# Turning 320 of 480 channels of the inverse spectrum by DMA through DRAM, in a replanned order, in a gated long-convolution and gMLP kernel

## The chip, the cores and the metric

The kernel runs on one core of a Trainium2 chip. A core has the engines PE (TensorE, matmul), DVE (VectorE), ACT (ScalarE), POOL (GpSimd) and SP (SyncE), which issue their instructions in order, each from its own queue, and share 16 DMA engines. The metric is the device time of one execution in microseconds (us); lower is better. Times are compared as medians of several executions.

## The reference

For x of 2048 positions and 640 channels the output is a mix of two branches, `g * a + (1 - g) * b`, with the gate `g = sigmoid(sum(x * gate_w))` per position.

Branch a is a long convolution of every channel with its own kernel of 2048 taps, which is itself computed from 128 complex modes per channel:

```python
P = jnp.exp(logdA[:, :, None] * l[None, None, :])
K = jnp.einsum('dn,dnl,dn->dl', Cc, P, dB).real
Kf = rfft of K padded to 4096;  Uf = rfft of u padded to 4096
y  = irfft(Uf * Kf)[first 2048] + u * Dskip
```

Branch b is a gMLP block: `z = gelu(x @ w_in)`, cut into halves of 864; the second half goes through a layernorm over channels, is mixed over positions by the 2048 x 2048 matrix `w_sp` plus `b_sp`, multiplied by the first half, and goes through `w_out`.

## The kernel before, in words

**Branch b** is `z2_tile` and `z1_tile` (projection and gelu; z1 goes to DRAM) and `sp_block`, eight blocks of 256 positions each: the mixing matmuls ps_g (L810), the gating on DVE (vT, L814 and L816), and the output projection ps_o (L830), rescaled into `acc` or `ob` (L834).

**Branch a** is a Fourier transform in two stages, done as matmuls with tables. The 640 channels are handled as two groups, `h=0` with 480 channels and `h=1` with 160. Exponentials and tables (`k_exps`, `k_tables`: ACT and DVE) feed `k_sub` (ps_k, L1043 and L1044), which gives factors of the kernel K. They go to DRAM (`KA_d`, `KB_d`), and `k_expand` loads them back in repeated form, 27 transfers for each group, into `xk`. `conv_s1` is stage 1 of K: matmuls ps_s1k (L1132), evacuated to bf16 by ACT or DVE (L420), stored to `FK_d`. `s1_u` does the same for the input (`FU_d`). The turn of axes between the stages is the trip through DRAM: `conv_s2` loads `fu` and `fk` back with other axes in the partitions.

`conv_s2` runs over 32 blocks of frequencies: one at a time for 480 channels (32 products in all), two at a time for 160 (16 products). For each step PE makes ps_u (L1179) and ps_s2k (L1186), ACT copies ps_u to `us` (L420), DVE multiplies ps_s2k by `us` (the product p, L1188), PE turns the product back by the first inverse stage (ps_v, L1194), and ACT copies ps_v into `vs[h]` (L1196), a bf16 tile of 128 partitions x 32 blocks x 480 or 160 channels.

`conv_vt` then turns `vs` in place. Within every group of 32 partitions the partition index and the block index change places. This is done by DVE with STREAM_TRANSPOSE (L1202) on 40 channels at a time, taken as 20 float32 pairs: 12 such operations for 480 channels and 4 for 160. Each needs all blocks of its group. `conv_i2` is the last inverse stage: matmuls with the table HT over the turned `vs` (L1278 for 480, L1276 for 160), half of them added to the output by DVE (L1210), half scaled by ACT (tm, L1227) and added by DVE or POOL (L1229); then the output goes out from SP. A block of `conv_i2` needs all turns of its group.

**What sets the order.** Nothing is ordered at run time. The class `Plan` collects all operations as tasks, with an assumed cost, the buffers that they read and write, and a priority: the longest remaining path, plus a bias, plus an entry of the table `TUNE`, keyed by function and line offset. `Plan.run` then simulates the engines, with one serial DMA channel and a fixed landing time for each transfer, and writes down a static sequence for each engine. A task whose engine is given as several (evacuations: ACT or DVE; transfers: `QQ`, SP or POOL) is given to one of them by this simulation. A change of `TUNE` or of an assumed cost therefore changes the order on all engines, and where such tasks run, and nothing of what is computed. The semaphore waits follow from the tiles that an instruction reads and writes in the emitted order; two accesses to one tile are ordered when their address ranges overlap.

Around the change: the `fu` and `fk` loads stand on SP only and have three buffers each; the transfers of `k_expand` and the stores to `FK_d` are on SP or POOL. The regions of memory for the second group (`cv1`) are opened once the first group's stage 1 is done.

Of the kernel before, what the change touches and what calls it, by code (L numbers as in the profile page):

```python
# [13 lines left out]
BF = mybir.dt.bfloat16  # L14
# [11 lines left out]
class Handle:  # L26
# [9 lines left out]


TUNE = {
    ('conv_s1', 15, ('g', 1)): 3463,
    ('conv_s2', 43, ('h', 0)): 2566,  # L40
    ('conv_s2', 34, None): 6794,
    ('conv_s2', 27, ('h', 1)): 252,
    ('conv_s2', 10, None): 10339,
    ('conv_s2', 14, ('h', 0)): 1700,
    ('conv_s2', 42, None): 26749,
    ('eights', 6, None): 35100,
    ('eights', 13, None): 2232,
    ('i2_out', 7, None): -1101,
    ('k_exps', 10, None): -17175,
    ('k_store', 13, None): -4187,  # L50
    ('k_store', 14, None): -20275,
    ('k_sub', 13, None): -11680,
    ('k_tables', 31, None): 12165,
    ('k_tables', 32, ('c', 2)): -15072,
    ('k_tables', 32, ('c', 6)): -5826,
    ('k_tables', 32, None): -8380,
    ('k_tables', 30, None): -26683,
    ('k_tables', 29, ('c', 7)): -19807,
    ('k_tables', 29, None): -21734,
    ('k_tables', 18, ('c', 7)): 1753,  # L60
    ('k_tables', 18, None): -14417,
    ('k_tables', 17, ('c', 3)): 17782,
    ('k_tables', 36, ('c', 6)): -8483,
    ('k_tables', 36, ('c', 7)): -31949,
    ('k_tables', 20, ('c', 1)): -27268,
    ('k_tables', 20, ('c', 4)): -2369,
    ('k_tables', 20, None): 1822,
    ('k_tables', 21, ('c', 4)): -3380,
    ('k_tables', 38, ('c', 2)): 2234,
    ('k_tables', 38, ('c', 6)): 23056,  # L70
    ('k_tables', 38, None): 275,
    ('k_tables', 23, None): 2152,
    ('main', 160, None): 9405,
    ('main', 350, None): -821,
    ('main', 151, ('g', 0)): 23897,
    ('main', 151, None): 1843,
    ('main', 149, None): 6466,
    ('main', 370, None): -29957,
    ('main', 365, None): -6662,
    ('main', 435, None): -1293,  # L80
    ('main', 415, None): -9571,
    ('main', 412, None): 12264,
    ('main', 443, None): -165,
    ('main', 411, None): -19156,
    ('main', 419, None): -2698,
    ('ob_load', 7, None): -17373,
    ('quads', 6, None): -20516,
    ('s1_u', 13, ('h', 1)): 20716,
    ('s1_u', 13, ('n0', 10)): -22604,
    ('s1_u', 16, None): -19744,  # L90
    ('s1_u', 3, ('n0', 0)): -12146,
    ('s1_u', 3, None): -2641,
    ('s1_u', 18, ('h', 1)): -36848,
    ('s1_u', 14, ('n0', 2)): 280,
    ('s1_u', 14, None): -34357,
    ('sp_block', 20, ('tb', 0)): 14608,
    ('sp_block', 20, ('tb', 1)): 2295,
    ('sp_block', 20, ('tb', 2)): 1783,
    ('sp_block', 20, ('tb', 7)): -4631,
    ('sp_block', 20, None): -28643,  # L100
    ('sp_block', 42, ('tb', 4)): -2761,
    ('sp_block', 42, None): -1053,
    ('sp_block', 47, None): -23570,
    ('sp_block', 3, ('tb', 0)): 4184,
    ('sp_block', 3, ('tb', 7)): -12304,
    ('sp_block', 3, None): -2466,
    ('sp_block', 8, None): -13804,
    ('sp_block', 6, ('tb', 2)): -1163,
    ('sp_block', 6, ('tb', 4)): -19214,
    ('sp_block', 6, None): -2088,  # L110
    ('sp_block', 5, ('tb', 2)): -12744,
    ('sp_block', 5, ('tb', 7)): -13832,
    ('z1_tile', 10, ('g', 1)): -8523,
    ('z1_tile', 10, None): 3231,
    ('z1_tile', 15, ('g', 0)): 2499,
    ('z1_tile', 15, None): -2684,
    ('z2_tile', 18, ('h', 1)): -15976,
    ('z2_tile', 18, None): 9745,
}
HELPERS = ("dma", "actf", "evac", "<lambda>", "ptt", "pts", "ftt", "fts", "pstt", "S_", "E", "K_", "M_")  # L120

# [1 line left out]
class Plan:  # L123
# [51 lines left out]
    def run(self):  # L175
# [26 lines left out]
        dma = 0.0  # L202
# [9 lines left out]
        while len(order) < N:  # L212
# [10 lines left out]
            while again:  # L223
                again = False
                for e in self.ENG:
# [3 lines left out]
                    for i in ready[e]:  # L229
                        if done[i] or rdy[i] > now + 1e-9:  # L230
                            continue
                        t = T[i]
                        ok = True
                        for h in t["hs"]:
# [3 lines left out]
                            n = self.rings[h.ring]  # L238
# [16 lines left out]
                    t = T[best]  # L255
                    i = best
# [3 lines left out]
                    c = t["costs"][t["engs"].index(e)]  # L260
# [15 lines left out]
                    if t["nb"]:  # L276
                        s = max(end + (0.0 if t["hold"] else 1.0), dma)
                        dma = s + t["nb"] / 1e6
                        fin = dma + (2.2 if t["hold"] else 0.9) + (0.9 if e == "POOL" else 0.0)
                        if t["hold"]:  # L280
                            end = dma
                    else:
                        fin = now + c + self.LAT.get(e, 0.0)
# [35 lines left out]
def kernel(  # L319
# [20 lines left out]
    P = 128  # L340
# [35 lines left out]
    dram = ctx.enter_context(tc.tile_pool(name="dram", bufs=1, space=DRAM))  # L376
    GW, GO = (480, 160), (0, 480)
    FU_d = [dram.tile([16, 4, 2, 32, w], BF, name=f"FU_d{w}") for w in GW]
    FK_d = [dram.tile([16, 4, 2, 32, w], BF, name=f"FK_d{w}") for w in GW]
    KA_d = [dram.tile([16, NB, w], BF, name=f"KA_d{w}") for w in GW]  # L380
    KB_d = [dram.tile([129, w], BF, name=f"KB_d{w}") for w in GW]
    z1_d = dram.tile([8, P, NFT, 256], BF, name="z1_d")
# [17 lines left out]
    def dma(q, out_, in_, nb, r=(), w=(), tr=False, bias=0.0, deps=(), run=640):  # L400

        qs = (q,) if isinstance(q, str) else q

        def fn(e):
            if tr:
                E_[e].dma_start(out=out_(), in_=in_(), transpose=True)  # L406
            else:
                E_[e].dma_start(out=out_(), in_=in_())
        return add(qs, [0.67 if tr else QC[x] + (0.3 if run < 250 and x == "SP" else 0.0) for x in qs], fn, r=r, w=w, nbytes=max(nb * 3.64e-6 if tr else nb / run * (20 + run / 27.2) / 16000, 0.001) * 1e6, hold=tr, bias=bias, deps=deps)
# [159 lines left out]
    X = {}  # L569
# [515 lines left out]
    def k_expand(h):  # L1085
        W = GW[h]
        xk = sbt((CVA, CV1)[h], f"xk{h}", "xk", [P, NS, W])
        rx = [("cva", "cv1")[h]]
        KA, KB = KA_d[h], KB_d[h]
        rd = KAB[h]  # L1090
        pieces = []

        def mk(src, dims):
            return bass.AP(src.tensor, src.offset, dims + [list(src.ap[-1])])
        x3 = lambda: xk()[:].rearrange("p (e r) d -> p e r d", e=2)

# [12 lines left out]
        wk = [[] for _ in range(NS)]  # L1109
        for i, (n0, rep, rows_, dst, src) in enumerate(sorted(pieces, key=lambda t: t[0])):  # L1110
            for n in range(n0, n0 + rep):
                wk[n].append((xk, i))
            dma(QQ, dst, src, rows_ * 2 * W, r=rd + rx, w=[(xk, i)], bias=8000 - 5 * i, run=2 * W)
        return xk, wk

    cva_ids = []
# [36 lines left out]
    def conv_s2(h):  # L1153
        W = GW[h]
# [5 lines left out]
        for k in range(0, 32, NK):  # L1160
# [33 lines left out]
                        pe.matmul(pv()[:, W * n:W * n + W], lhsT=GV(k + n, i), rhs=p12()[:, i, W * n:W * n + W], start=(i == 0), stop=(i == 1))  # L1194
            mv_id[h] = add("PE", 2 * NK * mm(W), mv_, r=[p12, gk], w=[pv], bias=S2B + 200)
            add("ACT", 0.15 + NW / 1170, lambda e, k=k, pv=pv: act.copy(out=X["vs"][h][:, k:k + NK, :], in_=pv()[:, 0:NW].rearrange("p (k d) -> p k d", k=NK)), r=[pv, "cvb"], w=[("vs", h, k)], bias=S2E)  # L1196

    def conv_vt(g):
        h = g // 3
# [47 lines left out]
    def conv_i2(h, oo):  # L1247
        W, dsl = GW[h], slice(GO[h], GO[h] + GW[h])
        nn = (1, 2)[h]
        for u, n in enumerate(range(0, NS, 2 * nn)):  # L1250
# [28 lines left out]
            if u == 0:  # L1279
# [95 lines left out]
```

## Time and profile before

| | |
|---|---|
| median of 8 runs | 357.6 us |
| runs, lowest to highest | 353.97 to 359.53 us |
| the profiled execution | 358.57 us, its span 356.8 us |
| mean TensorE clock granted | 0.964 |
| PE, DVE, ACT, POOL busy | 312.8, 282.5, 248.7, 85.8 us |
| moved by DMA | 59.89 MB, 168 GB/s |
| hardware queue, software queue | 62.7% and 6.5% of the 16 engines' span |
| first and last product of 480 channels (L1188) | starts at 266.7, ends at 305.9 us |
| turns on DVE (L1202) | 16, 18.7 us |

The profile is of one execution; all positions below are microseconds from the start of its span. "Busy" does not count the issue of DMAs, waits or branches. In the chain a line gives the start, the length and the work or the wait; in a group of instructions the columns after the bar are the busy time, the mean length of one in ns, and the idle time before them. "issue" is time in which an engine waited for nothing that the profile shows. A DMA time "to landing" runs from the issue to the completion.

### The profile page before, as it was taken

Reading aid. Unit: us, or ns where it says so; the run is one execution under the profiler, and the core shown is the slowest. Engines: PE = TensorE matmul, PEld = TensorE weight load, DVE = VectorE, ACT = ScalarE, POOL = GpSimd, SP = SyncE. Lnnn points to the kernel's source line nnn. Section 1 sums busy time; section 2 is a strip of 40 time slices with the busy share of each in tenths; the row PEclk is TensorE's granted clock in tenths of the full one; section 3 lists DMA queues with packets and bytes.
Section 4 is the critical chain, followed back from the end, with each engine's and each line's share of the span. In section 5 each row is a group of like instructions: output and inputs, shape, how many; then the busy total and the mean of one; then the engine's idle time right before and its main releaser. Section 6 shows DMA issues by size and latency. Waiting matters only on the chain.

```text
span 356.8 us, 8362 instructions
## 1 busy us (share of the span) xinstructions
PE 312.8 (88%) x3237; PEld 217.0 (61%) x3237; DVE 282.5 (79%) x554; ACT 248.7 (70%) x445; POOL 85.8 (24%) x108
## 2 busy tenths in 40 slices
PE   3899797988999999999999999499999999809982
PEld 3454353676775787878966988277775333406751
DVE  4049896597899789996699699237678999996985
ACT  1877666799999678889967574136648888804842
POOL 3002766000000000000270064436478000203220
PEclk9999999899999999999999999689999999976998
DMA  7989886757686669689088337977969786273404
GB/s 206 203 137 216 154 223 146 205 144 162 175 227 164 172 123 242 153 212 203 27 115 156 93 78 138 171 189 219 274 183 276 197 253 175 63 209 135 140 28 129
DMA packets 108848, 59.89 MB, mean 168 GB/s; under 512 B 76730, under 2 KB 105194, under 8 KB 108810
## 3 DMA queue, kind: packets, MB, share of 16 engines
q1 hardware_dynamic: 106218, 54.46, 62.7%
q0 software_dynamic: 2592, 4.91, 6.5%
q8 instruction: 25, 0.41, 0.5%
q14 instruction: 13, 0.11, 0.1%
HBM read 25.25 MB, written 19.47 MB: 125 GB/s over the span
## 4 chain that ended last, share of the span: by engine, by line
PE 28%; DVE 27%; ACT 18%; SPq 10%; DMA 7%; POOL 5%; issue 5%; ACTq 0%; DVEq 0%
PE ps_g L810 10%; ACT mr L413 9%; SPq L406 8%; DVE p L1188 6%; DVE vs L1202 5%; PE ps_z L622 4%; PE ps_o L830 4%; ACT L413 2%; PE ps_s2k L1186 2%; ACT ET L413 2%; DMA xk<-KA_d 2%; PE ps_v L1194 2%; DMA FK_d<-s1k 2%; POOL phi L359 2%; PE ps_s1k L1132 2%
## 5 line engine op out<-in xcount | busy, mean ns | idle before, releaser
L810 PE MATMUL ps_g<-wT,z2n 128*128 128x256 bf16 (+1 forms) x896 | 107.7, 275 | 4.0 <-DVE vT L814 2.1
L810 PEld LDWEIGHTS <-z2n 128*128 128x128 bf16 (+1 forms) x896 | 89.5, 102 | 20.9 <-issue 5.4
L1188 DVE TENSOR_TENSOR p<-ps_s2k,us 128x960 bf16<-128x960 f32 (+1 forms) x48 | 48.7, 1043 | 4.1 <-ACT us L420 1.5
L991 POOL COPY ET<-mr 128x80 bf16<-128x80 bf16 x7 | 6.0, 853 | 135.9 <-PE ps_k L1044 129.2
L830 PE MATMUL ps_o<-Wout,vT 128*128 128x320 bf16 (+1 forms) x224 | 34.0, 299 | 2.2 <-ACT s1u L420 1.8
L622 PE MATMUL ps_z<-xg,Win 128*128 128x512 bf16 (+1 forms) x140 | 33.3, 393 | 2.7 <-ACT zt L413 2.7
L590 PE MATMUL ps_z<-Win,xT 128*128 128x432 bf16 (+1 forms) x160 | 30.5, 347 | 2.0 <-ACT gl L596 2.0
L413 ACT ACTIVATE ET<-ci 128x640 bf16<-128x640 int16 (+1 forms) x40 | 25.7, 681 | 7.0 <-DVE ci L359 7.0
L1044 PE MATMUL ps_k<-ET 128*32 128x33 bf16 x640 | 28.0, 258 | 2.7 <-issue 2.7
L1043 PEld LDWEIGHTS <-ET 128*32 128x32 bf16 x640 | 27.0, 192 | 4.7 <-issue 4.4
L830 PEld LDWEIGHTS <-vT 128*128 128x128 bf16 (+1 forms) x224 | 21.8, 97 | 12.3 <-issue 3.2
L1196 ACT CAST vs<-ps_v 128x480 bf16<-128x480 f32 (+1 forms) x48 | 24.8, 520 | 5.0 <-PE ps_v L1194 4.7
L1043 PE MATMUL ps_k<-ET 128*32 128x33 bf16 x640 | 28.2, 259 | 0.0
L1044 PEld LDWEIGHTS <-ET 128*32 128x32 bf16 x640 | 27.4, 195 | 0.0
L1194 PE MATMUL ps_v<-p,G 128*128 128x480 bf16 (+1 forms) x128 | 25.6, 304 | 1.6 <-DVE p L1188 0.8
L814 DVE TENSOR_TENSOR vT<-ps_g,br 128x512 bf16<-128x512 f32 (+1 forms) x32 | 18.8, 617 | 10.1 <-PE ps_g L810 10.1
L622 PEld LDWEIGHTS <-Win 128*128 128x128 bf16 (+1 forms) x140 | 14.6, 104 | 19.4 <-issue 5.7
L420 ACT CAST us<-ps_u 128x480 bf16<-128x480 f32 (+1 forms) x48 | 24.5, 520 | 2.1 <-ACT vs L1196 0.9
L1186 PE MATMUL ps_s2k<-fk,T 128*128 128x480 bf16 (+1 forms) x128 | 25.4, 309 | 0.4 <-DMA fk<-FK_d 0.3
L590 PEld LDWEIGHTS <-xT 128*128 128x128 bf16 x160 | 15.5, 98 | 15.9 <-issue 2.5
L413 ACT ACTIVATE mr<-lre 128x320 bf16<-128x320 f32 x66 | 24.8, 456 | 0.0
L420 ACT CAST s1k<-ps_s1k 128x960 bf16<-128x960 f32 (+1 forms) x16 | 13.4, 860 | 13.0 <-PE ps_s1k L1132 10.1
(193 smaller groups left out, 588.6 us busy)
## 6 DMA issues: line engine op xcount, KB each, us to landing
FU_d<-s1u SPq DMA_DIRECT2D x16, 240.0 KB, 2.8
fu<-FU_d SPq DMA_DIRECT2D x16, 240.0 KB, 3.7
fk<-FK_d SPq DMA_DIRECT2D x16, 240.0 KB, 4.1
z_d<-zt SPq DMA_DIRECT2D x24, 128.0 KB, 1.9
z1t<-z_d SPq DMA_DIRECT2D x8, 384.0 KB, 4.4
xf<-in_A_u_dram SPq DMA_DIRECT2D x8, 320.0 KB, 3.3
Win<-in_B_w_in_dram SPq DMA_DIRECT2D x2, 1080.0 KB, 5.7
ob_d<-ob SPq DMA_DIRECT2D x12, 160.0 KB, 4.2
```

What stands on the lines that cost most here:

```text
L406: E_[e].dma_start(out=out_(), in_=in_(), transpose=True)
L413: return add("ACT", cost, lambda e: act.activation(out=out_(), in_=in_(), func=func, scale=scale), r=r, w=w, fset=fs, bias=bias, deps=deps ...
L420: (vec.tensor_copy if e == "DVE" else act.copy)(out=out_(), in_=in_())
L590: pe.matmul(ps()[:, h, 0:432 + h], lhsT=xT[:, i, 128 * st:128 * st + 128], rhs=Win2[:, i, 432 * h:432 * h + 432 + h], start=(i == 0), stop ...
L622: pe.matmul(ps()[0:fs, ft - f0, :], lhsT=Win1[:, i, 128 * ft:128 * ft + fs], rhs=xg()[:, i, :], start=(i == 0), stop=(i == ND - 1))
L810: pe.matmul(ps()[0:fs, ft - f0, :], lhsT=z2n[:, st, 128 * ft:128 * ft + fs], rhs=wT()[:, st, :], start=(st == 0), stop=(st == NS - 1))
L830: pe.matmul(ps()[:], lhsT=vT[ft // 2]()[0:fs, ft % 2, 128 * r:128 * r + 128], rhs=Wout[0:fs, ft, HD * h:HD * h + HD], start=(ft == 0), sto ...
L1043: pe.matmul(o_, lhsT=ET[:, 0:32, d], rhs=M2[:, :, d], start=True, stop=False, tile_position=(0, 32 * q))
L1044: pe.matmul(o_, lhsT=ET[:, NA:NA + 32, d], rhs=E2[:, :, d], start=False, stop=True, tile_position=(0, 32 * q))
L1186: pe.matmul(ps()[:, i, W * n:W * n + W], lhsT=TK(k + n, i), rhs=fk()[:, j + n, :], start=True, stop=True)
L1188: add("DVE", dv1(2 * NW), lambda e, p12=p12, ps=ps, us=us: vec.tensor_tensor(out=p12()[:, :, 0:NW], in0=ps()[:, :, 0:NW], in1=us()[:, 0:NW ...
L1194: pe.matmul(pv()[:, W * n:W * n + W], lhsT=GV(k + n, i), rhs=p12()[:, i, W * n:W * n + W], start=(i == 0), stop=(i == 1))
```

## The change

1. The table `TUNE` is replaced as a whole (some 88 entries). No operation comes from it, only another order.
2. In `Plan.run` the landing time assumed for a transfer grows from 0.9 to 1.3 us (transposing loads: 2.2 to 2.4), and the assumed cost of the transfers that expand K for 160 channels grows by half. Both act on the order alone.
3. Channels 0 to 319 of `vs[0]` are turned by DMA. After each fourth block of `conv_s2(0)` these channels of four blocks are stored to a new DRAM buffer `VK_d` (8 stores of 320 KB); a new function `conv_vd` loads them back into the same place of `vs[0]` with the partition and block indices swapped, by group of 32 partitions (16 loads of 160 KB, rows of 640 bytes). Channels 320 to 479 are still turned by DVE (4 operations in place of 12), and those of the second group too. A block of `conv_i2(0)` waits for the loads of its half of the blocks and for the four turns.

Its core (the entries of `TUNE` are left out):

```diff
-                        fin = dma + (2.2 if t["hold"] else 0.9) + (0.9 if e == "POOL" else 0.0)
+                        fin = dma + (2.4 if t["hold"] else 1.3) + (0.9 if e == "POOL" else 0.0)
...
+    VD = 320
+    VK_d = dram.tile([32, P, VD], BF, name="VK_d")
...
-            dma(QQ, dst, src, rows_ * 2 * W, r=rd + rx, w=[(xk, i)], bias=8000 - 5 * i, run=2 * W)
+            dma(QQ, dst, src, rows_ * (2, 3)[h] * W, r=rd + rx, w=[(xk, i)], bias=8000 - 5 * i, run=2 * W)
...
+            if h == 0 and k % 4 == 3:
+                dma(QQ, lambda k=k: VK_d[k - 3:k + 1, :, :].rearrange("k m d -> m k d"),
+                    lambda k=k: X["vs"][0][:, k - 3:k + 1, 0:VD], 1024 * VD,
...
+    def conv_vd():
+        NG = 2
+        g4 = 16 // NG
+        for m in range(NG):
+            for q in range(4):
+                for w in range(2):
+                    i0 = 16 * w + g4 * m
+                    dma(QQ, lambda q=q, i0=i0: X["vs"][0][32 * q:32 * q + 32, i0:i0 + g4, 0:VD],
+                        lambda q=q, i0=i0: VK_d[:, 32 * q + i0:32 * q + i0 + g4, :], 1024 * VD // NG,
+                        r=[("VK", i) for i in range(8)], w=[("vd", q, m, w)], bias=6500, run=640)
...
-            vk = [("va", 3, b) for b in range(4)] if h else [("va", g, b) for g in range(3) for b in range(4)]
+            vk = [("va", 3, b) for b in range(4)] if h else [("va", g, b) for g in range(VD // 160, 3) for b in range(4)] + [("vd", q, n // 8, w) for q in range(4) for w in range(2)]
...
-    for g in range(3):
+    conv_vd()
+    for g in range(VD // 160, 3):
         conv_vt(g)
```

In the built program all eight stores to `VK_d` are on POOL; of the loads nine are on SP and seven on POOL.

More of the change, by code (lines that the diff above doesn't have):

```diff
@@ L38 @@
 TUNE = {
[L39 to L118, printed above, removed]
+    ('conv_i2', 37, ('h', 0)): 1844,
+    ('conv_i2', 39, ('h', 1)): -2564,
+    ('conv_i2', 39, None): -6223,
+    ('conv_s2', 43, None): -17523,
@@ new lines @@
+    ('conv_s2', 35, ('h', 0)): 633,
+    ('conv_s2', 35, ('h', 1)): 993,
+    ('conv_s2', 34, ('h', 0)): 24993,
+    ('conv_s2', 34, None): -4152,
+    ('conv_s2', 27, ('h', 0)): 2880,
+    ('conv_s2', 14, None): -40,
+    ('conv_s2', 28, None): -7269,
+    ('conv_s2', 42, None): -2974,
+    ('conv_vt', 4, None): -1249,
+    ('eights', 6, None): -4248,
+    ('i2_out', 7, None): -4434,
+    ('k_exps', 7, None): 83,
+    ('k_exps', 10, ('c', 0)): -406,
+    ('k_exps', 10, ('c', 4)): 573,
+    ('k_store', 14, None): -2870,
@@ new lines @@
+    ('k_store', 6, ('h', 1)): -12388,
+    ('k_store', 6, None): 8586,
+    ('k_sub', 23, None): -10732,
+    ('k_sub', 13, None): -11315,
+    ('k_tables', 31, ('c', 3)): 220,
+    ('k_tables', 31, ('c', 5)): 1445,
+    ('k_tables', 31, ('c', 7)): -6456,
+    ('k_tables', 41, None): -2285,
+    ('k_tables', 30, ('c', 3)): -7154,
+    ('k_tables', 29, ('c', 1)): 6497,
+    ('k_tables', 29, ('c', 2)): -3535,
+    ('k_tables', 29, ('c', 4)): -18229,
+    ('k_tables', 29, None): -762,
+    ('k_tables', 18, None): -19435,
@@ new lines @@
+    ('k_tables', 17, ('c', 2)): -12249,
+    ('k_tables', 17, ('c', 4)): -5119,
+    ('k_tables', 36, None): -11081,
+    ('k_tables', 20, ('c', 0)): -19918,
+    ('k_tables', 20, None): 6756,
+    ('k_tables', 21, None): -17729,
+    ('main', 153, ('g', 0)): 386,
+    ('main', 153, None): 1913,
+    ('main', 157, None): 1007,
+    ('main', 151, None): 3607,
+    ('main', 359, None): 1898,
+    ('main', 371, None): -18999,
+    ('main', 434, None): -211,
+    ('main', 417, None): 337,
+    ('main', 421, None): -10346,
@@ new lines @@
+    ('main', 426, None): -4607,
+    ('quads', 6, None): -3335,
+    ('s1_u', 13, ('n0', 0)): 3712,
+    ('s1_u', 13, ('n0', 2)): -778,
+    ('s1_u', 13, ('n0', 8)): 1854,
+    ('s1_u', 13, None): -10863,
+    ('s1_u', 16, ('h', 1)): -4227,
+    ('s1_u', 20, ('h', 1)): -1896,
+    ('s1_u', 3, ('n0', 0)): -2236,
+    ('s1_u', 3, None): 1530,
+    ('s1_u', 18, None): -4151,
+    ('s1_u', 14, None): -38867,
+    ('sp_block', 23, ('tb', 2)): 2780,
+    ('sp_block', 25, ('tb', 4)): -4691,
+    ('sp_block', 25, ('tb', 6)): -3589,
@@ new lines @@
+    ('sp_block', 25, ('tb', 7)): -3310,
+    ('sp_block', 25, None): -634,
+    ('sp_block', 20, ('tb', 5)): 5109,
+    ('sp_block', 20, None): -7447,
+    ('sp_block', 42, None): -17740,
+    ('sp_block', 47, None): -17689,
+    ('sp_block', 3, ('tb', 0)): 6151,
+    ('sp_block', 3, ('tb', 1)): 5386,
+    ('sp_block', 3, None): -4487,
+    ('sp_block', 8, None): -8681,
+    ('sp_block', 6, ('tb', 3)): -4753,
+    ('sp_block', 6, None): 7590,
+    ('sp_block', 5, None): 5037,
+    ('tg_build', 9, ('c', 1)): -7818,
@@ L119 @@
+    ('x_group', 3, None): 1651,
+    ('z1_tile', 10, None): 1132,
+    ('z1_tile', 15, ('g', 1)): 2402,
+    ('z2_tile', 18, ('h', 1)): -17771,
 }
@@ L1196, in conv_s2 @@
             add("ACT", 0.15 + NW / 1170, lambda e, k=k, pv=pv: act.copy(out=X["vs"][h][:, k:k + NK, :], in_=pv()[:, 0:NW].rearrange("p (k d) -> p k d", k=NK)), r=[pv, "cvb"], w=[("vs", h, k)], bias=S2E)
+            if h == 0 and k % 4 == 3:
+                dma(QQ, lambda k=k: VK_d[k - 3:k + 1, :, :].rearrange("k m d -> m k d"), lambda k=k: X["vs"][0][:, k - 3:k + 1, 0:VD], 1024 * VD, r=[("vs", 0, k - z) for z in range(4)], w=[("VK", k // 4)], bias=S2B, run=2 * VD)
+    def conv_vd():
[5 more added lines that the diff above has]
+                    i0 = 16 * w + g4 * m
+                    dma(QQ, lambda q=q, i0=i0: X["vs"][0][32 * q:32 * q + 32, i0:i0 + g4, 0:VD], lambda q=q, i0=i0: VK_d[:, 32 * q + i0:32 * q + i0 + g4, :], 1024 * VD // NG,
+                        r=[("VK", i) for i in range(8)], w=[("vd", q, m, w)], bias=6500, run=640)
     def conv_vt(g):
```

## The prediction

> **What bounds the kernel now.** I read the page's top first, then its chain, then stretches of 20 us of the span, then the waits of the last 57 us.
>
> ```profile
> span 356.8 us, 8362 instructions
> PE 312.8 (88%) x3237; PEld 217.0 (61%) x3237; DVE 282.5 (79%) x554; ACT 248.7 (70%) x445; POOL 85.8 (24%) x108
> ```
>
> PE leads on average, but the limit changes by stage (columns: PE, PEld, DVE, ACT, POOL busy us, granted clock, DMA share, GB/s):
>
> ```profile
> 220.00:240.00 20.00, 14.79 (x296) 10.87 (x297) 9.03 (x13) 6.35 (x9) 8.99 (x16) 0.74 0.95 196
> 280.00:300.00 20.00, 19.27 (x88) 7.68 (x87) 19.15 (x18) 17.30 (x35) 0.00 (x0) 1.00 0.80 229
> 300.00:320.00 20.00, 10.42 (x59) 5.15 (x57) 19.53 (x19) 10.18 (x20) 1.81 (x2) 0.93 0.46 116
> 320.00:340.00 20.00, 17.92 (x161) 13.13 (x161) 16.54 (x22) 12.67 (x31) 5.46 (x5) 0.82 0.43 145
> ```
>
> From 120 to 220 us PE is full (19.4 to 20 us of each 20). At 220 to 240 it idles 5.2 us until the expansion of K lands. Then comes stage 2 of the 480 channels: 32 products on DVE (L1188), first at 266.7 us, last ending at 305.9. DVE paces it: 36.9 of those 39.2 us are these products, 0.39 + 0.39 + 0.48 are three other operations. After it DVE alone turns the spectrum while PE waits. The chain shows that (start, us, what):
>
> ```profile
> 304.77 1.17 DVE p L1188
> 305.98 0.58 PE ps_v L1194 x2
> 306.87 0.82 DVE s1k L420
> 307.76 1.03 issue
> 308.80 12.77 DVE vs L1202 x11
> 321.61 1.76 PE ps_i L1278 x4
> ```
>
> and so do the waits (who, for whom: us, times, longest) and the groups:
>
> ```profile
> PE ps_i L1278 <- DVE vs L1202: 9.4, 1, 9.4
> ...
> POOL FK_d L408 <- ACT s1k L420: 33.7, 2, 33.4
> ```
>
> ```profile
> L1202 DVE STREAM_TRANSPOSE vs<-vs 128x640 f32<-128x640 f32 x16 | 18.7, 1290 | 0.0
> ```
>
> Sixteen turns cost 18.7 us, 1.17 each; twelve are the 480 channels'. The last DVE operation ends at 353.4 and the last output transfer 3.4 us later. I call the first product T0 (266.7) and the end of the 32nd P0 (305.9): P0 to the end is 50.9 us.
>
> **What the Trainium skill says.** "VectorE: DVE Perf Modes", section "The three transpose paths": DVE turns 32x32 blocks only. So a turn never mixes groups of 32 partitions, and a plain transfer can do it by swapping two axes, one group per load. "DMA: Bandwidth & Descriptors", "Anatomy of one DMA — SWDGE (gpsimd) path": fixed latency is near 2 us, mostly the completion's receipt, and a wait is held by the issuing sequencer, so what stands behind it waits too. The trace agrees: transfers of 240 KB land in 2.8 to 4.1 us, and POOL stood 33.4 us at one store. Same page, "Issuing engines are not separate DMA queues": all issuers share the 16 engines. "TensorE: Matmul & The Clock Gate", "Part 1: The HAM clock gate": after an idle window TensorE drops to half clock; the first L1278 matmuls after the 9.4 us wait took 604 ns each, their median is 366.
>
> **The change, part by part.** All estimates are on the profiled run: 358.57 us, of which 356.8 are span and 1.8 lie around it; the median of the runs is 357.6, 1.0 below.
>
> *Removed:* 8 of 12 turns, 8 x 1.163 = 9.3 us of DVE, all on the path, since PE waited 9.38 us there. But that gap also covered the 160 channels' round trip: their FK_d stores were issued at 309.8 to 311.4, their fk loads landed at about 323. A mere removal would expose that wait. So what the order does with the 160 channels decides.
>
> *New order* (table, landings, the last expansion's cost; one answer together). Read from the two built programs with the old durations: PE has 196.1 us of work ahead of the first stage 1 matmul before, 192.6 after; DVE 0.4 us and ACT 4 us less. Ahead of the first stage 2 matmul PE has 221.3 in both. The cover while xk lands (from the end of the sixth k_sub) grows from 15.7 to 17.1 us against 5.2 us of idle at half clock. I take T0 1.5 us earlier; nothing shows the landings of another order, so −4 to +4.
>
> *The moves on each queue.* The 160 channels' expansion is 27 transfers; 13 of SP's were spread among the fu and fk loads, now 16 stand in one block behind the sixth pair of these loads (of 16), and 11 are on POOL ahead of everything added there. SP issues one in 0.36 us, so the block holds the seventh pair back 5.8 us. The sixth can be issued about 5 us after T0, when PE has read the third; the seventh then at T0 + 11, landed at T0 + 15 (fk takes 4.1). Its first reader is the 13th product, which stands behind 12 products (13.8) and four evacuations (3.3): hidden with 2 us to spare; that cover gone, DVE waits by the lateness. POOL's 11 issues (0.8 each, 9 us) end before the stage 1 of the 160 channels needs the rows: this stage 1 now lies inside the stage 2 of the 480, and nothing but the FK_d stores waits for it. Six of its eight evacuations go to DVE, which had two. DVE from T0 to P0 is then 36.9 products + 6 x 0.82 evacuations + 3 x 0.55 rescalings of ps_o + 0.8 for G and 0.3 for vT = 44.5; with the 1.1 us of idle that the stage had before, 45.7. That is +6.5. Bounds: +5.3 without idle, +8.5 if transfers fall behind. ACT gets lighter by as much, but isn't the limit.
>
> *Added:* 8 stores to VK_d (320 KB) on POOL, issued where a copy of vs frees them, 0.8 us each, queue otherwise idle for 33 us. The 160 channels' FK_d stores sit between them: each waits at most for the next four blocks (4.6 us), and has the rest of the stage as cover. The packets are 640 B; the trace's packet records have 44 ns (median) for 960 B and 20 for 320 B, so about 40 ns: 4096 packets over 16 engines are 1.25 us a store, 10 us in all, and 10 for the 16 loads. DMA was busy 31 of 40 us in this stage; 31 + 7 stores x 1.25 + 5.5 for the moved FK_d traffic = 45 of 46. Full, but not yet the limit.
>
> *Waits that the change adds.* Columns 0 to 319 and 320 to 479 of vs share one tile, with rows that interleave. In the built program each in-place turn waits on overlapping address ranges, not on its own columns. DVE's first of the four turns left (three products of the 160 after P0) waits until all eight VK_d stores land; the first nine vd loads (5 SP, 4 POOL) wait for the third turn; the fourth turn waits until those nine land; the other seven wait for it. Behind them stand the products of the 160 on DVE, and on SP the eighth fu load and all outputs.
> - Turn 1: ACT's copy ends 1.6 us after P0 (product to copy in the trace), issue 0.8, landing 3.5 (2.8 as the quickest 240 KB store, 6.1 as the FK_d stores from POOL): P0 + 5.9. DVE has 3 x 0.82 = 2.5 us: it stands 3.4 (2.7 to 6).
> - Turns 1 to 3 with three products: 3 x 1.17 + 3 x 0.82 = 6.0, so P0 + 11.9.
> - Nine loads are 1.4 MB. The fk loads of 160 channels, 1.3 MB, landed in 4.5 to 5.5 us, into 128 partitions. These write 32 partitions each; I take 5.6 of packets + 2 of landing and issue = 7.7, so P0 + 19.6. DVE's cover is two products, 1.65: it stands 6 (4 to 14: xk's loads into 16 to 64 partitions had 114 ns per 960 B packet, 2.6 times the median).
> - Then turn 4 (1.2), six products (4.9), and the last part: inverse stage, four turns of the 160 (4.7), output, 18 us with gaps as now. DVE ends at P0 + 44.3, the kernel at P0 + 47.7, before 50.9: −3.2.
>
> Sum: −1.5 + 6.5 − 3.2 = +1.8, so 360.4 on the profiled run, less 1.0 is 359.4 on the median.
>
> **The rivals.**
> - *Faster.* The stalls are nearly hidden and the order gains its 4 us. For: 9.3 us of DVE go, and DVE's whole work from T0 to the end falls from 81.8 to 77.3. Against: the waits above stand in the program. Time: T0 −4 (2.5 better), stalls 0.7 and 1.8 shorter (landing 2.8; nine loads as the fk loads), no idle in stage 2 (1.1): 359.4 − 6.1 = 353.3.
> - *Slower, by one mechanism: the nine vd loads that the fourth turn waits for.* For: xk's 114 ns. Then 5.6 us of packets become 14.6; less 1 that lies under issuing, +8 on the path: 367.4. It decides when these loads land over 9.5 us after the third turn, where I have 7.7. Against: nine loads cover all four groups of 32 partitions at once.
> - *Transfers crowd stage 2* (45 of 46 us). Fu and fk come late, P0 +2 and T0 late by 0.6: 363.5. For: 229 GB/s at share 0.80 already; against: SP has three tiles of lead.
> - *It doesn't do what it says:* the turn goes to DMA, but DVE's saved 9.3 us return as evacuations (+3.3), rescalings and stalls (9.4). This is my forecast rather than a rival: the 18.7 us turn row halves and the end doesn't move.
>
> **How the numbers follow.** Forecast (359.4, its own 356.4 to 362.5) 0.5, of which 0.33 within 1%, 0.03 faster, 0.14 slower; faster 0.2 (0.14 and 0.06 within); vd loads 0.2, all slower; crowding 0.1 (0.08 and 0.02 within). Together faster 0.17, same 0.41, slower 0.42. One per cent, 3.6 us, is about what a measurement of this kernel tells from no change (runs lie between 353.97 and 359.53). Range 352.5 to 367.0: it leaves out about a tenth on each side, namely a larger gain in T0, and the upper half of the vd rival.
>
> **What would show it.** Right: eight turns, some 9.4 us; T0 near 265; 45 to 46 us from T0 to P0; DVE waits of 3 to 4 us for VK_d and 6 for the vd loads before turns; PE's 9.4 us wait replaced by one as long for these. Wrong: DVE busy through the tail; T0 off by over 4; fk or fu named as what DVE or PE wait for; a DMA share of 1.0 in stage 2.

## The result, and the profile after

The changed kernel takes 371.1 us (median of 11 runs, 365.4 to 377.3), the kernel before 356.9 us beside it. The ratio is 1.036, with a 95% interval of 1.030 to 1.042: slower by 3.6%. The prediction was 359.4 us, with a range up to 367.0. Ratios here leave disturbed runs out, so they are not the ratios of the medians. The first profile is of one of the longest executions (377.0 us), so I show a second one of the same kernel, of 369.8 us, and name the first where it differs.

The top of the page and, below it, the two stretches that the prediction summed, from the first product of 480 channels (T0) to the end of the 32nd (P0), and from there to the end; the last line is the first stretch in the kernel before. (The cut at 315.2 is 0.2 us early: the 32nd product ends at 315.4.) Columns: PE, PEld, DVE, ACT, POOL busy us, granted clock, DMA share, GB/s.

```profile
span 368.0 us, 8387 instructions
PE 315.9 (86%) x3237; PEld 222.6 (60%) x3237; DVE 280.1 (76%) x556; ACT 243.2 (66%) x434; POOL 95.2 (26%) x121
```

```profile
266.60:315.20 48.60, 40.84 (x205) 19.24 (x204) 41.62 (x45) 33.29 (x66) 16.38 (x23) 1.00 0.88 266
315.20:368.00 52.80, 31.25 (x236) 23.64 (x236) 30.92 (x45) 20.40 (x48) 12.77 (x16) 0.79 0.50 127
...
266.70:305.90 39.20, 37.70 (x184) 16.25 (x181) 36.48 (x37) 33.46 (x67) 8.33 (x15) 1.00 0.79 212
```

So the stage grew by 9.6 us, from 39.2 to 48.8, and both engines, at 93 to 96% before, are now at 84 to 86%. The tail is 52.6 us, 1.7 more than before, with 11 us less of DVE work in it. T0 has not moved: 266.6 against 266.7. Together 11.2 us, the difference of the spans. (In the longer execution T0 is at 274.4; on the way there PE waits 3.4 us for xk loads, which it does not in the second one, and idles 4.5 us in a place that the profile names "issue" and that takes 2.2 us in the second one. The stage is 48.2 and the tail 52.6 us, as here. Two executions of one kernel differ by this, so the change alone doesn't explain it.)

The tail, DVE's own sequence (start, length, operation, count; in brackets the idle time before it and what ended it):

```profile
320.81 1.27 DVE L1217 STREAM_TRANSPOSE vs<-vs 128x640 f32<-128x640 f32 x1 [2.83 <-DMA VK_d<-vs]
321.98 0.78 DVE L1191 TENSOR_TENSOR p<-ps_s2k,us 128x640 bf16<-128x640 f32 x1
322.68 1.29 DVE L1217 STREAM_TRANSPOSE vs<-vs 128x640 f32<-128x640 f32 x1
323.86 1.51 DVE L1191 TENSOR_TENSOR p<-ps_s2k,us 128x640 bf16<-128x640 f32 x2
325.29 1.30 DVE L1217 STREAM_TRANSPOSE vs<-vs 128x640 f32<-128x640 f32 x1
326.46 1.72 DVE L1191 TENSOR_TENSOR p<-ps_s2k,us 128x640 bf16<-128x640 f32 x2
336.40 1.27 DVE L1217 STREAM_TRANSPOSE vs<-vs 128x640 f32<-128x640 f32 x1 [8.21 <-DMA vs<-VK_d]
```

Both waits that the prediction read out of the built program are there, in their places: 2.8 us for the stores, 8.2 for the loads. PE waits with DVE (for whom: us, times, longest), which has taken the place of the 9.4 us that it waited for the twelve turns:

```profile
PE ps_v L1197 <- DVE p L1191: 13.0, 3, 8.9
...
DVE vs L1217 <- DMA vs<-VK_d: 8.2, 1, 8.2
```

### The profile page after: what moved, and what is told of

It reads as the page before. It is cut to its first block, busy times and chain, and to the rows that moved or that the text cites. A ratio compares the mean times of both kernels' runs of the same rounds, so it can differ in the third digit from the quotient of the medians.

```text
span 375.2 us, 8387 instructions
## 1 busy us (share of the span) xinstructions
PE 317.3 (85%) x3237; PEld 223.7 (60%) x3237; DVE 280.0 (75%) x556; ACT 243.5 (65%) x434; POOL 95.3 (25%) x121
## 3 DMA queue, kind: packets, MB, share of 16 engines
q1 hardware_dynamic: 106994, 54.69, 59.9%
## 4 chain that ended last, share of the span: by engine, by line
PE 47%; SPq 14%; ACT 12%; DVE 10%; DMA 10%; issue 5%; POOL 1%; DVEq 0%; ACTq 0%
PE ps_g L813 16%; SPq L409 12%; PE ps_o L833 6%; PE ps_z L625 5%; DVE p L1191 5%; ACT mr L416 5%; PE ps_k L1046 4%; PE ps_k L1047 3%; PE ps_v L1197 3%; PE ps_s2k L1189 3%; DMA xk<-KA_d 3%; PE ps_s1k L1135 2%; DMA vs<-VK_d 2%; SPq L411 2%; DMA KA_d<-kf 2%
## 5 line engine op out<-in xcount | busy, mean ns | idle before, releaser
L813 PE MATMUL ps_g<-wT,z2n 128*128 128x256 bf16 (+1 forms) x896 | 111.4, 280 | 3.7 <-DVE vT L817 3.6
L813 PEld LDWEIGHTS <-z2n 128*128 128x128 bf16 (+1 forms) x896 | 91.3, 104 | 23.3 <-issue 7.3
L1191 DVE TENSOR_TENSOR p<-ps_s2k,us 128x960 bf16<-128x960 f32 (+1 forms) x48 | 47.7, 1037 | 8.2 <-PE ps_s2k L1189 4.3
L1197 PE MATMUL ps_v<-p,G 128*128 128x480 bf16 (+1 forms) x128 | 27.6, 326 | 15.2 <-DVE p L1191 13.0
L994 POOL COPY ET<-mr 128x80 bf16<-128x80 bf16 x6 | 7.7, 1282 | 128.6 <-PE ps_k L1047 96.7
L423 ACT CAST us<-ps_u 128x480 bf16<-128x480 f32 (+1 forms) x48 | 24.1, 521 | 22.8 <-PE ps_u L1182 13.5
L625 PE MATMUL ps_z<-xg,Win 128*128 128x512 bf16 (+1 forms) x140 | 31.4, 379 | 1.6 <-ACT zt L416 1.2
L1046 PEld LDWEIGHTS <-ET 128*32 128x32 bf16 x640 | 27.2, 192 | 4.3 <-issue 3.9
L1197 PEld LDWEIGHTS <-G 128*128 128x128 bf16 x128 | 12.2, 109 | 24.9 <-DVE p L1191 16.8
L423 ACT CAST s1k<-ps_s1k 128x960 bf16<-128x960 f32 (+1 forms) x11 | 9.9, 911 | 24.0 <-PE ps_s1k L1135 22.2
```

The source lines that it names most:

```text
L423: (vec.tensor_copy if e == "DVE" else act.copy)(out=out_(), in_=in_())
L625: pe.matmul(ps()[0:fs, ft - f0, :], lhsT=Win1[:, i, 128 * ft:128 * ft + fs], rhs=xg()[:, i, :], start=(i == 0), stop=(i == ND - 1))
L813: pe.matmul(ps()[0:fs, ft - f0, :], lhsT=z2n[:, st, 128 * ft:128 * ft + fs], rhs=wT()[:, st, :], start=(st == 0), stop=(st == NS - 1))
L1046: pe.matmul(o_, lhsT=ET[:, 0:32, d], rhs=M2[:, :, d], start=True, stop=False, tile_position=(0, 32 * q))
L1191: add("DVE", dv1(2 * NW), lambda e, p12=p12, ps=ps, us=us: vec.tensor_tensor(out=p12()[:, :, 0:NW], in0=ps()[:, :, 0:NW], in1=us()[:, 0:NW ...
```

## The experiments

Each kernel keeps the exact sequence of instructions of one of the two kernels on all engines, except for what is named. Theory and rival changed on the way, so each expectation names its own.

| run | what | time, us | ratio to before (95%) |
|---|---|---|---|
| after_again | the changed kernel | 374.6 | 1.040 (1.028 to 1.051) |
| order_only | new order, no DMA turn | 369.5 | 1.016 (1.004 to 1.028) |
| turn_only | old order, DMA turn | 368.2 | 1.027 (1.018 to 1.035) |
| planes | changed kernel, vs in three planes | 359.3 | 0.995 (0.991 to 0.999) |
| loads_after_turns | changed kernel, loads behind the turns | 365.2 | 1.020 (1.009 to 1.032) |
| layout_only | kernel before, three planes | 355.7 | 0.997 (0.994 to 1.001) |
| turn_planes | old order, DMA turn, three planes | 365.4 | 1.030 (1.022 to 1.037) |
| turn_early | the same, loads ahead of fk's | 367.4 | 1.030 (1.022 to 1.038) |
| turn_early1 | the same, 160 channels by DMA | 359.9 | 1.010 (1.007 to 1.013) |
| planes_act | planes, evacuations on ACT | 359.6 | 1.007 (1.003 to 1.010) |
| early_loads | planes, fu and fk earlier on SP | 356.5 | 0.996 (0.991 to 1.000) |
| early_both | and ps_u one product earlier | 357.4 | 1.003 (0.998 to 1.009) |
| early_both2 | and ps_u two products earlier | 354.8 | 0.996 (0.993 to 1.000) |

The medians of the kernel before, beside them, were 355.3 to 359.1 us. Three more ran once each: no_s1k (353.8 us) and no_s1k_no_xk (351.0 us), which leave work out, so that their traces count and not their times, and early_us1 (361.2 us). Positions and waits are read from one trace of each kernel.

### Order or turn

The changed kernel again gave the second profile; its expectation was

> The changed kernel once more, for a second profile. If the profile on record is typical in its shape: first product of the 480 channels at 271 to 275 us (266.7 before), 47 to 49 us to the end of the 32nd (39.2 before), a DVE wait of about 3 us for the VK_d stores and of about 8 us for the vd loads; ratio to before 1.03 to 1.045. If that profile showed a disturbed run, the first product is near 267 and the stage near 45.

The stage and the waits came out as expected, T0 did not: it is at 266.6. The late T0 belongs to that one execution.

For the order alone, the stores and loads are dropped from the changed kernel, and DVE does the eight other turns ahead of its first one:

```diff
-  dma(QQ, lambda k=k: VK_d[...], ...)        # and the vd loads
+  no transfer is issued
-  vec.transpose(out=w32(b), in_=w32(b))      # first turn of 480 channels
+  eight turns of channels 0 to 319, then this one
```

> The changed kernel's order on every engine, with all twelve turns of the 480 channels on DVE again and no transfer to or from VK_d (eight turns stand in front of the first of the four left; all else in the same sequence). Theory 'order': the loss of 13 to 14 us lies in the new order ahead of the turns; time 367 to 372, ratio 1.03 to 1.04. Theory 'turn by DMA': the loss lies in the traffic and in the waits on it; without them 358 to 362, ratio at most 1.015, though DVE has 9.3 us more to do.

Ratio 1.016, between the two theories; stage 48.1 us, tail 46.8 us, no wait for a transfer to or from VK_d. For the turn alone, the kernel before gets the stores, and in place of its eight turns the loads, behind the four that are left:

```diff
-  twelve turns of 480 channels on DVE
+  POOL: store four blocks of vs to VK_d when their copies are issued
+  four turns on DVE, then sixteen loads, alternately SP and POOL
```

> The kernel before with its own order on every engine, where eight of its twelve turns are taken out and the eight VK_d stores (on POOL as the copies of vs finish) and sixteen loads (half SP, half POOL, behind the four turns left) put in. Theory 'order': the DMA turn alone is about neutral, since the loads land about when the twelve turns ended: 356 to 362, ratio 1.0 to 1.015. Theory 'turn by DMA': 366 to 371, ratio 1.025 to 1.04, with the products of stage 2 held up by late fu and fk loads.

Ratio 1.027, in the range of the theory of the DMA turn, but not by its mechanism: the stage is 39.0 us, so no product is held up, and the tail is 59.9 us. Each part costs by itself, in its own place: the order 8.9 us of stage (it gives 4.0 back in the tail), the DMA turn 9.0 us of tail. The two stages also answer the rival of crowded transfers. In the old order the stage is 39.0 us with all 2.6 MB of stores in it, and in the new order it is 48.1 us without any: the stores delay nothing.

### The waits nobody wrote

The 480 channels of vs are laid out as three planes of 160, so that the turned plane and the two that go through DRAM have separate addresses. A store becomes two, one for each plane.

```diff
-  X["vs"] = [tg.tile([P, 32, w], BF, name=f"vs{w}") for w in GW]
+  X["vs"] = [tg.tile([P, 3, 32, 160], BF, ...), tg.tile([P, 1, 32, 160], BF, ...)]
-  VK_d = dram.tile([32, P, VD], BF, name="VK_d")
+  VK_d = dram.tile([2, 32, P, 160], BF, name="VK_d")
```

> The changed kernel in its order, with vs of the 480 channels laid out as three planes of 160 channels, so that the turned plane and the two planes that go through DRAM share no range of addresses; the built program then has no wait of a DVE turn on VK_d stores or vd loads (each store is issued as two of 160 KB). Theory 'waits nobody wrote': DVE's 11 us of waits before turns go, the products of the 160 channels run through, 6 to 10 us faster than the changed kernel: 361 to 365. Rival: the inverse stage needs the loads anyway, and they land no earlier: 368 to 371.

Ratio 0.995: about 4% faster than the changed kernel, more than expected, and level with the kernel before (the medians of all runs are 359.3 and 359.1 us). The turns run through, and six products behind the fourth follow at once:

```profile
320.69 1.27 DVE L1217 STREAM_TRANSPOSE vs<-vs 128x640 f32<-128x640 f32 x1
321.87 1.50 DVE L1191 TENSOR_TENSOR p<-ps_s2k,us 128x640 bf16<-128x640 f32 x2
323.30 1.27 DVE L1217 STREAM_TRANSPOSE vs<-vs 128x640 f32<-128x640 f32 x1
324.49 1.50 DVE L1191 TENSOR_TENSOR p<-ps_s2k,us 128x640 bf16<-128x640 f32 x2
325.91 1.27 DVE L1217 STREAM_TRANSPOSE vs<-vs 128x640 f32<-128x640 f32 x1
```

The tail falls from 52.6 to 40.4 us, the stage stays at 48.1. The two waits are 11.0 of these 12.2 us. The layout changes the packets too: on SP they are of 2560 bytes at 176 ns in place of 640 at 49 ns, so nine loads take 6.3 us of the sixteen engines and not 7.1. But the loads didn't land quicker: those on SP have a median of 7.9 us to landing here (all sixteen at once) against 4.4 in the changed kernel. Nor is it the layout as such:

> Control: the kernel before, order and all twelve turns on DVE as they are, with vs of the 480 channels in three planes. If the layout has no price or gain of its own (copies, turns and matmuls on rows of 160): ratio 0.995 to 1.005, turns at 1.17 us each. Rival: the layout itself makes turns or matmuls quicker and is part of what the three planes brought: 0.985 or less.

0.997 with the kernel before: as good as no effect.

Half the remedy is to keep the layout and issue all sixteen loads behind the fourth turn, so that no turn waits for a load:

```diff
-  nine loads behind the third turn, seven behind the fourth
+  sixteen loads behind the fourth turn
```

> The changed kernel with its layout of vs and its order, but the sixteen vd loads are issued behind the fourth turn instead of nine behind the third and seven behind the fourth, so that no turn waits for a load. Theory 'the wait stands in front of other DVE work': DVE's 8 us wait goes and six products run while the loads fly, though they land 3 us later; the 3 us wait for the VK_d stores stays: ratio 1.015 to 1.03, against 1.036 to 1.04 of the changed kernel. Rival 'the loads set the end anyway': 1.035 to 1.045, with PE waiting for the loads.

Ratio 1.020, as the theory said. The 8.2 us wait is gone, that for the stores stays at 3.2, and a wait for the inverse stage, which needs the later loads, comes to 4.0:

```profile
DVE wT L1225 <- PE ps_u L1293: 4.0, 1, 4.0
...
DVE vs L1217 <- DMA VK_d<-vs: 3.2, 1, 3.2
```

### The turn in the old order

The same planes in the order of the kernel before:

> The order of the kernel before with eight turns by DMA, as in the run that did the turn alone, but with vs in three planes so that turns and transfers don't wait for each other. Theory: the DMA turn gains nothing in that order, since its round trip (stores 5 us, loads 8 us or more behind the last copy) is as long as the turns it replaces and nothing is left to do meanwhile, the 160 channels' stage 1 coming only then: ratio 0.99 to 1.01. Rival 'only the waits cost': 9 us faster than before, ratio 0.975 to 0.985.

Ratio 1.030, no better than with the false waits: theory and rival both missed. DVE's turns are done at 308.8 us, and then everything stands:

```profile
DVE wT L1229 <- PE ps_i L1297: 22.0, 2, 21.6
PE ps_i L1297 <- DMA vs<-VK_d: 19.9, 1, 19.9
```

SP's queue shows one reason:

```profile
306.55 1.58 SPq L408 DMA_DIRECT2D FK_d<-s1k  x2
315.10 0.81 SPq L408 DMA_DIRECT2D fk<-FK_d  x2
316.15 9.72 SPq L1223 DMA_DIRECT2D vs<-VK_d  x8
```

The eight vd loads stand behind two fk loads that wait until 315.1 us for the FK_d stores. Putting all loads ahead of the fk loads:

> The order of the kernel before with eight turns by DMA and vs in three planes, and the sixteen vd loads issued ahead of the 160 channels' fk loads, behind their FK_d stores (in the run with three planes in the old order the eight on SP stood behind two fk loads that waited for the FK_d stores). Theory 'queue place': the 21.6 us wait of DVE falls to 10 to 13 us, the inverse stage starts some 10 to 11 us earlier than there, ratio 0.99 to 1.005 in place of 1.030. Rival 'the loads themselves are slow': ratio 1.02 or more.

1.030 again, as the rival said, so the place in the queue was not the reason either, or not the only one: DVE still waits 17.9 us. Now the loads take 10.0 (POOL) and 11.6 us (SP) to land, in company with the FK_d stores, and the four fk loads behind them 9.9. With half the bytes (one plane by DMA, eight turns on DVE):

> As the run with early loads, but only 160 of the 480 channels go through DRAM (half the bytes; eight turns on DVE instead of four, in a stretch where DVE has nothing else). Theory: turns and transfers end together, 11 to 12 us behind the last product of 480 channels where the twelve turns ended 15.6 behind it; the 160 channels' products still wait for their own round trip: ratio 0.985 to 0.995. Rival 'the round trip of the 160 channels sets it': 0.998 to 1.01.

1.010, at the edge of the rival's range; DVE's wait is 7.0 us. The expectation of a gain fell, the direction held: less through DRAM is less loss. In this order the 160 channels' stage 1 comes after P0, so DVE and PE have nothing to do while both round trips fly. That the two hinder each other on the DMA engines is likely from the landing times, but no run separates them.

### Where the stage's 9 us come from

First I took the moved evacuations off DVE:

```diff
-  evac(("ACT", "DVE"), ...)    # stage 1 of 160 channels
+  the same place in the sequence, always on ACT
```

> The kernel with three planes, with all eight evacuations of the 160 channels' stage 1 on ACT (six were on DVE), in the same places of the sequence. Theory 'DVE's work sets stage 2': 6 x 0.81 = 4.9 us leave DVE there; the stage of 480 channels shrinks from 48.8 to 44 or 45 us and the ratio to before from 0.995 to 0.98 to 0.985. Rival 'the sequence makes the gaps': matmuls of ps_o and ps_s1k stand on PE between two ps_s2k, ps_s1k takes one of the two buffers of ps_s2k, and ACT's extra work delays us; the stage stays at 48 us, DVE idles more (10 us in place of 6), ratio 0.99 to 1.0.

The rival held for the stage (its ratio, 0.99 to 1.0, is missed at 1.007). The stage of the planes kernel and of this one (DVE 4.6 us less busy, the stage no shorter):

```profile
268.20:316.30 48.10, 40.68 (x205) 19.25 (x204) 41.86 (x46) 33.52 (x66) 21.63 (x30) 1.00 0.91 267
```

```profile
267.60:316.00 48.40, 41.21 (x205) 19.24 (x204) 37.24 (x39) 36.46 (x72) 21.73 (x30) 1.00 0.90 264
```

DVE does not set this stage any more. The ends of the products show where it stands. Counted from the first one's start, the 12th ends at 15.6 us (15.9 before), the 13th at 22.1 (17.0 before): 5 of the 9 us are lost in one place, the rest in small steps behind it. From the start of the 12th to the end of the 13th PE does 17 ps_o and ten ps_s1k matmuls, DVE four evacuations and two rescalings. I left the stage 1 of the 160 channels out:

> The kernel with three planes in the changed order, without the stage 1 of the 160 channels: its sixteen ps_s1k matmuls and eight evacuations are left out (POOL fills s1k with zeros, so those channels' spectrum of K is not computed); all else in the same sequence. Theory 'two buffers': ps_s1k takes one of the two ps_s2k buffers eight times, and each time the next ps_s2k waits for a product to end; without it the stage of 480 channels falls from 48.8 to 40 to 43 us and DVE's idle in it from 6 to 2 us. Rival 'late ps_u': the gaps come from where ps_u and us stand in the sequence; the stage stays at 45 us or more with 6 us idle or more.

The theory of the two buffers fell: 13th product at 22.3, stage 48.5 us. Now PE waits for a transfer in that place:

```profile
286.02 1.03 PE L1182 MATMUL ps_u<-fu,T 128*128 128x480 bf16 x3 [1.13 <-DMA fu<-FU_d]
```

So a second thing was hidden there. In the planes kernel SP's queue between the sixth pair of loads and the seventh (T0 is 268.2):

```profile
273.36 0.32 SPq L411 DMA_DIRECT2D fk<-FK_d  x1
273.84 2.20 SPq L411 DMA_DIRECT2D xk<-KA_d  x5
276.14 0.64 SPq L411 DMA_DIRECT2D xk<-KB_d  x1
276.82 4.80 SPq L411 DMA_DIRECT2D xk<-KA_d  x10
281.73 1.32 SPq L411 DMA_DIRECT2D fk<-FK_d  x3
283.10 1.49 SPq L411 DMA_DIRECT2D fu<-FU_d  x3
```

The block of expansion loads takes 7.8 us, and the seventh fu load, behind three fk loads, goes out no earlier than T0 + 14.9. Without these loads too:

> As the run without the 160 channels' stage 1, and without the 27 transfers that expand K for these channels (16 of them stand in one block on SP, between the sixth and the seventh pair of fk and fu loads); those channels' spectrum of K is not computed, all else is in the same sequence. In every kernel with the changed order the 13th product of 480 channels ends 15.7 us after the first began and the 14th at 22.1 to 22.9 us, with stage 1 or without. Theory 'two things in one place': the block on SP holds back the seventh pair, and stage 1 with 21 ps_o matmuls fills the same stretch; with both gone the 14th product ends at 18 to 19.5 us (ps_o remains) and the stage is 45 to 46.5 us in place of 49. Rival 'the sequence alone': 21.5 us or later, stage 48 us or more.

(The expectation counts the products one too high: they are the 12th and the 13th.) The 13th ends at 21.0, the stage is 45.8 us: stage as the theory said, 13th product between the two. But the seventh fu load still goes out late, at T0 + 14.1 (T0 is 265.0). In SP's queue in that trace

```profile
270.12 8.92 SPq L411 DMA_DIRECT2D fk<-FK_d  x4
279.09 1.44 SPq L411 DMA_DIRECT2D fu<-FU_d  x3
```

the three fk loads ahead of it wait for buffers that PE frees, the last of them until T0 + 13.7. So what makes this load late is its place behind three fk loads, with or without the block. Then the two causes were mended one by one, by moving tasks in the emitted sequence:

```diff
+  early_loads: each fu, fk load to behind the PE operation that frees its buffer
+  early_us1:   ps_u and us of product k to behind product k - 1
+  early_both, early_both2: both, with k - 1 and k - 2
```

> The kernel with three planes in the changed order; each fu and fk load of the 480 channels is moved up on SP to stand behind the operation that frees its buffer, so that fk and fu alternate and the seventh pair stands inside the block of expansion loads rather than behind it. PE, DVE and ACT keep their sequence. Theory 'SP': the 13th product ends at 18 to 20 us after the first began (22.1 before, 17.1 in the old order), stage 44 to 46 us (47.9), ratio 0.98 to 0.99. Rival 'PE sequence': 13th product at 21.5 us or later, stage 47 us or more, ratio 0.99 to 1.0.

> The kernel with three planes in the changed order; from the ninth product of 480 channels on, ps_u and its copy us are moved up to stand behind the issue of the product before (or behind their own loads and tables), loads on SP as they were. Theory 'SP': the seventh fu load lands too late for it, 13th product at 21 us or later; the later gaps of 2 us go, stage 45 to 47 us. Rival 'PE sequence': 13th product at 18 to 20 us, stage 43 to 45 us.

> Both edits: loads alternate on SP, ps_u stands behind the issue of the product before. If both causes together make the gap: 13th product at 17.5 to 19.5 us, stage 42 to 44.5 us, ratio 0.975 to 0.985. If neither does (stage 1 and ps_o on PE, 7 us, and DVE's evacuations are the load itself): stage 46 us or more, ratio 0.99 or more.

> As the run with both edits, with ps_u two products ahead instead of one (where buffers allow). If one product ahead still leaves DVE waiting for us, this is 1 to 2 us faster than it; if not, the same within 1 us, or slower by up to 2 us where ps_u waits for a buffer and holds up PE.

The loads alone change nothing (the seventh fu load goes out at T0 + 6.1, and the 13th product still ends at 22.1, as the rival said); ps_u alone makes it worse, since PE, in order, now waits 5.1 us for the fu load (13th at 29.0). Both together give 21.5 and a stage of 46.7 us; two ahead gives 22.7 and 47.6. So neither queue place is what remains: with loads and us in time, the 13th product still waits behind the matmuls of PE and the evacuations put there, and the late fu load is hidden under them as they are hidden under it. Mending one shows the other. The two moves shorten the stage by 1.4 us, and the kernel's time doesn't show it (1.003).

The rest of the 9 us is not explained by the amount of work. With planes PE has 3.0 us more of it in the stage than before and DVE 5.3 (40.7 and 41.8 against 37.7 and 36.5); without the 160 channels' stage 1 and expansion loads it is 0.8 and 0.9 more, and the stage is still 6.6 us longer than before, with both engines idle for over 7 us of it. What is left is where the same kinds of work stand in the sequence, such as the ps_o matmuls in front of the 13th product (17 here, not the 21 that an expectation above names). That is argued, not shown: no run has the stage 1 out and the fu loads early at once, and none moves the ps_o matmuls.

None of these versions is clearly quicker than the kernel with planes alone.

## Why the prediction was wrong

- *Removed turns.* Right: eight turns left, 9.9 us, and PE's 9.4 us wait gone. Right too that the order decides what that is worth: in the new order, where the 160 channels' products fill the round trip, the DMA turn without the added waits beats DVE turns (tail 40.4 against 46.8 us); in the old one it loses 3%.
- *T0.* Predicted 1.5 us earlier, within −4 to +4; measured the same in the second profile. It isn't earlier in the other traces either: 265.4 to 268.5 in after_again, order_only, planes, planes_act, early_both and early_both2, and 262.8 to 267.4 in the six of the old order. The prediction took the 5.2 us that PE idles before T0 for a wait for xk; of these, 2.7 us stand in front of ps_k and are named "issue", and only 2.5 wait for xk.
- *The stage, predicted 45.7 us, measured 48.8.* This step failed in its mechanism, not only in size. It summed DVE's work and gave it the old idle time of 1.1 us. DVE's work was even less than predicted (41.8 against 44.5), the idle 7 us: DVE waited 4.4 us for the copies us and 2.3 for ps_s2k. Taking 4.6 us of its work away moved nothing. The sentence that should have warned me was my own: the seventh pair "hidden with 2 us to spare". The block took 7.8 us and not 5.8 (0.5 us an issue, where I took 0.36), fu stands behind three fk loads and went out at T0 + 14.9 and not T0 + 11, and the 13th product came at 22.1 to 22.8 us, where my own figures put its end at 18.3. The late load alone isn't it either (issued early, the 13th product still ends at 22.1): what I took as DVE's cover stood on PE too, which was 96% full in that stage (37.7 of 39.2) and takes its matmuls in order. How the 9 us divide between these stays open beyond the 1.4 that the two moves gave back.
- *The tail, predicted 47.7 us, measured 52.6.* This is the other step that failed, and the larger part of the miss; its mechanism was right, each wait in its place, and its terms were too small. Store wait 3.4 predicted, 2.8 measured. Load wait 6 predicted, 8.2 measured: the nine loads landed 9.7 us behind the third turn, where I had 7.7 and had named 9.5 as the point from which they decide. The 640-byte packets took 49 ns on average, near the 40 assumed and far from the 114 that the rival feared; the loads issued by POOL are recorded in larger pieces, most of 4480 bytes at 328 ns, which is nearly the same per byte. So sixteen loads took 12.5 us of the sixteen engines in place of 10. The rest, 3 us, is an undercount from the fourth turn on: 27.6 us from its start to the last DVE operation, where the terms 1.2, 4.9 and 18 make 24.1 (the sum up to P0 + 44.3 has 24.7, a slip). Planes without any wait has 27.2, so it is not the waits.
- *What the prediction took from the Trainium skill.* Its page "DMA: Bandwidth & Descriptors", section "Anatomy of one DMA — SWDGE (gpsimd) path", says that a wait for a semaphore happens on the issuing sequencer, before the transfer is handed on. SP's queue agrees: in turn_planes the eight vd loads went out only behind two fk loads that waited until 315.1 us. The page "TensorE: Matmul & The Clock Gate", section "Part 1: The HAM clock gate", says that after an idle window TensorE falls to half clock. In the second profile PE did nothing from 329.5 to 338.4 us, and the granted clock was 0.50 from 332 to 342, where six products took 6.4 us that take 4.9 at full clock in the planes kernel. It agrees; the prediction had left these 1.5 us out of the waits' price.
- *A reading that doesn't come out of the traces.* The "faster" rival lets DVE's work from T0 to the end fall from 81.8 to 77.3 us. In the traces DVE is busy for 78.5 us there before and 72.5 in the changed kernel. More fell than was forecast, and it gained nothing.
- *The rivals.* The slower one by the loads came true in part; crowding of stage 2 by the stores is refuted; "faster" would have needed both a tail as in planes and a stage that stays at 39 us, and no run has both.

## What to carry to other kernels

Before costing a transfer into part of a tile, read which waits the built program gets from address ranges: here two unrelated parts of one tile, interleaved in memory, made an in-order engine wait 11 us, and separate planes took it off. A transfer round trip in place of engine work pays only where other work is placed under it, and the move of that work has its own price. The price of work moved into a stage can't be summed on the engine that paced the stage before: here DVE got 5 us more work, the stage grew by 9, and taking the work off DVE again changed nothing. Follow each in-order queue up to the first reader.

## What the runs showed that was not expected

One delay hid another in the same place: leaving out the work that filled PE there gained nothing until a block of sixteen DMA issues was gone as well (stage 48.5, then 45.8 us). And moving ps_u ahead without its load cost 6 us of stage (54.1 against 48.1).
